# Weight sums on VectorE without GpSimd, w_in kept as float32 in DRAM and read back

## The chip, the cores and the metric

The kernel runs on one core of one Trainium2 chip. The metric is device time in microseconds (us) of one execution, the median over several. A profiled execution gives the trace. Engines are named TensorE (PE, with PEld for its weight loads), VectorE (DVE), ScalarE (ACT), GpSimd (POOL) and SyncE (SP, which issues nearly all DMAs here).

## The reference, cut to what matters

A decayed linear attention over 4 batches, 8 heads, 768 positions of 64 columns gives `x` (3072 tokens of 512 columns). Then a feed-forward block with 2048 hidden columns follows. Inputs are of float64 for the two weights, float32 else:

```
out[:, :, sl] = intra + inter                  # blocks of 64 positions, a state per head
x = attn_out.transpose(0, 2, 1, 3).reshape(B * S, H * D)
h = np.maximum(x @ w_in, 0.0)                  # 3072 x 512 @ 512 x 2048
return (h * h @ w_out).astype(np.float32)      # 3072 x 2048 @ 2048 x 512
```

## The kernel before

**Split products.** A float32 number is split in a high and a low half that TensorE takes as float32r; a product is three matmuls (high x high, high x low, low x high). So each operand is split: ScalarE copies the high half out (`gh`, `part`, `v`, ...), VectorE subtracts it for the low half (`gl` at L760, L813, L925).

**Tokens.** 24 chunks of 128 tokens. The first eight form three plain tiles of 3, 3 and 2 chunks; each goes through 16 feed-forward steps `f` (function `ffn`): a product with w_in (L742), ReLU, square, split (ScalarE L756 to L759, VectorE L760), then products with w_out for `gh` (L748, L749) and `gl` (L751). The other 16 chunks are two groups of eight, which use 7 products in place of 8 for 2 x 2 blocks of matrices (L473). Those need sums and differences of weight blocks.

**Weights.** 16 parts of w_in and 16 of w_out arrive as float64 words (`work<-w`, 512 KB each, three buffers), and `weights` converts each: ScalarE L446, VectorE L447 to L453, which leaves float32 in a buffer `m` (three of them), then the halves (ScalarE L457, VectorE L459). This takes until 128 us, beside the first two tiles.

**Differences.** `differences(i, j, key)` makes, for each pair of parts (i = 0 for w_in, 1 for w_out; j = 0 to 7), what the groups of eight need, and stores it in DRAM (`kept`, 256 KB a block). Unchanged halves are stored from where they lie (`kept<-wi`, `kept<-wo`). GpSimd adds high and low to float32 again (L800, two of 128x512) in two buffers `ob`, makes four differences (L809, 128x256), and ScalarE and VectorE split each (L812, L813) into one of four `part` buffers (`v` in the later ones). For i = 0 this may begin in the second tile, for i = 1 when the third ends. The groups' products read the blocks back by `b<-kept` (L848), six buffers ahead.

**Visits.** Attention for later chunks is done in pairs, called visits, between feed-forward steps: chunk loads (`ka<-ka`, `qv<-qv`, 512 KB), 64x64 matmuls (L473), VectorE work on the results (L522, L549 to L558, L582) and, for the groups of eight, sums of chunks (`pairs`, L834) and their halves `pa`, `pz`, `ps`, `pt` (L826, L827).

**Order.** A planner (`Plan.order`) walks through all operations with durations and keys written in the code, and of those that could start next on an engine takes the one with the smallest key. What comes out is a fixed order for each engine. At run time each engine takes its instructions in that order and waits for what each needs. A key is thus a priority, not a time: an operation whose engine is free and whose inputs are there goes at once.

The function `differences` stands for GpSimd's whole work after the tables of the first 10 us.

Of the kernel before, what the change touches and what calls it, by code (L numbers as in the profile page):

```python
# [19 lines left out]
P = 128  # L20
# [208 lines left out]
PARTED = {1: 1, 2: 1, 4: 1, 5: 1, 6: 1, 7: 1, 8: 1}  # L229
BETWEEN = {3: 3, 4: 8, 5: 12}  # L230
APART, LATER_BY = 3, 4
# [3 lines left out]
FIRST_ORDER = [1, 2, 6, 5, 7, 4, 3]  # L235
PARTS = 8
AT_ONCE = [1, 2, 4, 6, 5, 7, 3]
LAST_ORDER = [4, 1, 2, 6, 5, 7, 3]
# [44 lines left out]
def kernel(ctx: ExitStack, tc: tile.TileContext, ka, qv, lamx, w, out):  # L283
# [71 lines left out]

    kept = [tc.dram_tile([NF // 2, P, 2, 7, 2 * P], F32, name=f"kept{i}") for i in range(2)]
    make("part", REGIONS["part"][0], [2, 2 * P], F32R)
    make("b", REGIONS["b"][0], [2, 2 * P], F32R)
# [66 lines left out]
    def weights(f, i, key, load_key):  # L425
# [32 lines left out]
        oh.late = f >= F_LATE  # L458
        ol = add("DVE", tt(512), lambda: nc.vector.tensor_tensor(out=part(1), in0=at(m), in1=part(0), op=ALU.subtract), [oh], [m])  # L459
        for o in (oh, ol):  # L460
            plan.use(f"{('wi', 'wo')[i]}{f}", o)
# [13 lines left out]
    class Chunk:  # L475
# [20 lines left out]
        def load(self, key):  # L496

            def part(buf, src, ps, size):
                o = in_turn("load", plan.op("SP", LOAD, key, lambda: loaded(nc.sync.dma_start(out=at(buf)[:, ps], in_=src[self.i][:, ps]), size), [], [buf]))
                o.size, o.slack = size, SLACK * (self.i >= N_ALONE + 6)  # L500
                return o
# [277 lines left out]
    def differences(i, j, key):  # L779
# [9 lines left out]
        def store(c, n, get, deps, bufs, uses):  # L789
            stored[i, j].append(plan.op("SP", LOAD, key, lambda: nc.sync.dma_start(  # L790
                out=kept[i][j][:, :, c:c + n].rearrange("p t c k -> p t (c k)"), in_=get().bitcast(F32)), deps, bufs, lat=2.9, uses=uses))
# [4 lines left out]
        else:  # L796
            store(0, 1, lambda: flat[0][:, :, 0:2 * P], w0[:2], [], names[:1])
            store(1, 1, lambda: flat[1][:, :, 0:2 * P], w1[:2], [], names[1:])
            store(6, 1, lambda: flat[1][:, :, 2 * P:], w1[:2], [], names[1:])
        prev = [plan.op("POOL", 1.38, key, lambda r=r, a=a: nc.gpsimd.tensor_tensor(  # L800
            out=at(r), in0=a[:, 0].bitcast(F32), in1=a[:, 1].bitcast(F32), op=ALU.add), list(w[:2]), raws, gate, uses=(name,))
            for r, a, w, name in zip(raws, flat, (w0, w1), names)]

# [4 lines left out]
        for c, (out_, a, b) in zip((2, 4, 5, 3), ((0, 2, 0), (2, 3, 2), (3, 3, 0), (1, 1, 3))):  # L808
            o = plan.op("POOL", 0.84, key, lambda out_=out_, a=a, b=b: nc.gpsimd.tensor_tensor(out=side(out_), in0=side(a), in1=side(b), op=ALU.subtract), prev, raws)  # L809
            part = Buf(kind)  # L810
# [39 lines left out]
    def first_products(p, j, key):  # L850
# [20 lines left out]
        def block(k, t, f, a, deps):  # L871
            b = h[t, f]
            o = plan.op("DVE", tt(WIDE) + 0.1, key - 6, lambda: nc.vector.tensor_tensor(out=at(b), in0=at(banks[k]), in1=at(a), op=ALU.add), deps, [banks[k], b, a])  # L873
            if p == 0 and k == "z":
                made[t, f] = [plan.op("DVE", tt(WIDE) + 0.1, key, lambda: nc.vector.scalar_tensor_tensor(
                    out=at(b), in0=at(b), scalar=0.0, in1=at(b), op0=ALU.max, op1=ALU.mult), [o], [b])]
                return o
            o1 = plan.op("ACT", act(WIDE) + 0.12, key, lambda: nc.scalar.activation(at(b), at(b), AF.Relu), [o], [b])  # L878
            o1 = plan.op("ACT", act(WIDE) + 0.12, key, lambda: nc.scalar.activation(at(b), at(b), AF.Square), [o1], [b])  # L879
            made[t, f] = [o1]  # L880
            return o
# [195 lines left out]
    for i in range(2):  # L1077
        for j in range(NF // 2):
            differences(i, j, 480 + 9 * j if i == 0 else 618 + 6 * j)

# [138 lines left out]
```

## Time and profile before

| what | value |
|---|---|
| median of 3 runs | 576.63 us (575.06 to 578.34) |
| profiled execution, own time | 575.11 us |
| its span, first to last instruction | 573.3 us |
| TensorE busy | 553.9 us, 97% |
| VectorE busy | 434.5 us, 76% |
| ScalarE busy | 330.2 us, 58% |
| GpSimd busy | 103.8 us, 18% |
| mean rate of the queues | 239 GB/s |

The span is the time from the first to the last instruction; 1.8 us of the execution's own time lie around it. Busy time counts an engine's instructions without the waits before them. A matmul's recorded duration overlaps the next one's, so the busy time is that of their union. In a timeline, the idle time of the engine ahead of an instruction stands in brackets behind it, with what ended it.

### The profile page before, as it was taken

How to read it: one execution, taken by the hardware profiler on the slowest of the kernel's cores; microseconds unless marked ns; L12 is line 12 of the kernel's file. 1: busy time of each engine (PE TensorE's matmuls, PEld its weight loads, DVE VectorE, ACT ScalarE, POOL GpSimd, SP SyncE). 2: the span in 40 equal slices, each digit the busy share in tenths (PEclk: the TensorE clock that was granted, in tenths of full speed). 3: DMA queues.
4: the chain of work that ended last, by engine and by line, in shares of the span. 5: the costliest groups of instructions: out<-in, count | busy, mean ns of one | idle time of the engine just before them, and what ended most of it. 6: DMA issues, size and time to landing. Idle time of an engine off the chain costs nothing.

```text
span 573.3 us, 12872 instructions
## 1 busy us (share of the span) xinstructions
PE 553.9 (97%) x4907; PEld 468.7 (82%) x4907; DVE 434.5 (76%) x778; ACT 330.2 (58%) x676; POOL 103.8 (18%) x106
## 2 busy tenths in 40 slices
PE   8999999999989889999998999999999999999997
PEld 7898899998869778787786788888878888888885
DVE  5998999984778999867478599999822323999664
ACT  5865676763544545556565655555446767754542
POOL 3000000004574674036666000000000000000000
PEclk9999999999989999999999999999999999999999
DMA  8999799854668558589999945676776776767765
GB/s 340 348 338 288 240 285 297 288 185 157 219 232 274 158 215 300 182 274 305 361 301 344 285 137 156 196 229 193 237 243 195 191 196 191 195 191 212 215 192 183
DMA packets 104397, 137.17 MB, mean 239 GB/s; under 512 B 7056, under 2 KB 88976, under 8 KB 104336
## 3 DMA queue, kind: packets, MB, share of 16 engines
q1 hardware_dynamic: 104192, 136.34, 75.1%
q8 instruction: 39, 0.64, 0.5%
q14 instruction: 22, 0.18, 0.1%
q10 hardware_dynamic: 144, 0.01, 0.0%
HBM read 100.67 MB, written 35.65 MB: 238 GB/s over the span
## 4 chain that ended last, share of the span: by engine, by line
PE 69%; DMA 16%; DVE 9%; issue 2%; POOL 1%; ACT 1%; SPq 1%; ACTq 0%; DVEq 0%
PE bank L473 52%; PE bank L742 8%; DMA b<-kept 6%; DMA qv<-qv 4%; PE bank L751 3%; PE bank L749 3%; PE bank L748 3%; DMA ka<-ka 2%; DMA work<-w 2%; DMA work<-qv 1%; DVE part L813 1%; DVE gl L760 1%; POOL ob L800 1%; DMA out<-work 1%; DVE pa L827 1%
## 5 line engine op out<-in xcount | busy, mean ns | idle before, releaser
L473 PE MATMUL bank<-v,b 128*128 128x512 f32 x672 | 153.4, 389 | 0.0
L473 PEld LDWEIGHTS bank<-v,b 128*128 128x128 f32 x672 | 126.0, 188 | 26.3
L924 ACT CAST v<-h 128x512 fp32r<-128x512 f32 x112 | 67.4, 621 | 58.4 <-PE bank L473 36.7
L873 DVE TENSOR_TENSOR h<-bank,u 128x512 f32<-128x512 f32 x64 | 44.0, 690 | 72.1 <-ACT u L869 42.2
L925 DVE TENSOR_TENSOR v<-h,v 128x512 fp32r<-128x512 f32 x112 | 75.2, 689 | 18.9 <-ACT v L924 9.6
L473 PE MATMUL bank<-pa,b 128*128 128x512 f32 x192 | 49.4, 392 | 4.3 <-DMA b<-kept 3.4
L800 POOL TENSOR_TENSOR ob<-wi 128x512 f32<-128x512 f32 x16 | 24.3, 1534 | 152.8 <-ACT work L756 127.6
L878 ACT ACTIVATE h<-h 128x512 f32<-128x512 f32 x56 | 35.4, 632 | 28.2 <-DVE h L873 26.2
L748 PE MATMUL bank<-wo,gh 128*128 128x512 f32 x125 | 49.7, 398 | 1.6 <-ACT gh L759 1.2
L473 PE MATMUL bank<-ps,b 128*128 128x512 f32 x192 | 49.1, 391 | 0.5 <-DMA b<-kept 0.4
L749 PE MATMUL bank<-wo,gh 128*128 128x512 f32 x125 | 49.1, 393 | 0.2 <-DVE wo L459 0.2
L869 ACT COPY u<-bank 128x512 f32<-128x512 f32 x48 | 28.0, 584 | 35.4 <-PE bank L473 35.3
L473 PE MATMUL bank<-pt,b 128*128 128x512 f32 x192 | 46.7, 391 | 1.1 <-DMA b<-kept 1.1
L473 PEld LDWEIGHTS bank<-pa,b 128*128 128x128 f32 x192 | 35.6, 188 | 13.3 <-DMA b<-kept 2.6
L473 PEld LDWEIGHTS bank<-pt,b 128*128 128x128 f32 x192 | 35.8, 188 | 8.9 <-issue 1.5
L932 DVE TENSOR_TENSOR h<-h,h 128x512 f32<-128x512 f32 x64 | 42.9, 686 | 0.1
L473 PEld LDWEIGHTS bank<-ps,b 128*128 128x128 f32 x192 | 35.7, 188 | 8.8 <-ACT v L812 0.9
L742 PE MATMUL bank<-xb,wi 128*128 128x384 f32 x192 | 35.2, 336 | 0.0
L879 ACT ACTIVATE h<-h 128x512 f32<-128x512 f32 x56 | 34.4, 627 | 0.6
L742 PEld LDWEIGHTS bank<-xb,wi 128*128 128x128 f32 x192 | 33.6, 188 | 0.9
L742 PE MATMUL bank<-xa,wi 128*128 128x384 f32 x180 | 34.1, 338 | 0.0
L742 PEld LDWEIGHTS bank<-xa,wi 128*128 128x128 f32 x180 | 31.6, 188 | 1.4 <-issue 0.2
(148 smaller groups left out, 959.8 us busy)
## 6 DMA issues: line engine op xcount, KB each, us to landing
b<-kept SPq DMA_DIRECT2D x224, 256.0 KB, 3.5
work<-w SPq DMA_DIRECT2D x32, 512.0 KB, 4.8
ka<-ka SPq DMA_DIRECT2D x24, 512.0 KB, 5.3
qv<-qv SPq DMA_DIRECT2D x20, 512.0 KB, 5.9
kept<-part SPq DMA_DIRECT2D x32, 256.0 KB, 3.5
kept<-v SPq DMA_DIRECT2D x32, 256.0 KB, 5.0
kept<-wo SPq DMA_DIRECT2D x24, 256.0 KB, 3.7
kept<-wi SPq DMA_DIRECT2D x8, 512.0 KB, 4.3
```

Source lines behind the costliest of these rows:

```text
L473: nc.tensor.matmul(*args, **kw, skip_group_check=True)
L742: nc.tensor.matmul(at(h)[:, 0:n], wt[:, cc, :], xt[:, cc, :], start=k == 0, stop=k == 3 * NCC - 1)
L748: nc.tensor.matmul(at(os_[j]), at(gh)[:, sl], woh[f], start=f == 0 and ti >= SINGLE, stop=False)
L749: nc.tensor.matmul(at(os_[j]), at(gh)[:, sl], wol[f], start=False, stop=False)
L800: prev = [plan.op("POOL", 1.38, key, lambda r=r, a=a: nc.gpsimd.tensor_tensor(out=at(r), in0=a[:, 0].bitcast(F32), in1=a[:, 1].bitcast(F32 ...
L869: return plan.op("ACT", act(WIDE) + 0.09, key - 6, lambda: nc.scalar.copy(at(dst), at(banks[k])), [o], [banks[k], dst])
L873: o = plan.op("DVE", tt(WIDE) + 0.1, key - 6, lambda: nc.vector.tensor_tensor(out=at(b), in0=at(banks[k]), in1=at(a), op=ALU.add), deps, [ ...
L878: o1 = plan.op("ACT", act(WIDE) + 0.12, key, lambda: nc.scalar.activation(at(b), at(b), AF.Relu), [o], [b])
L879: o1 = plan.op("ACT", act(WIDE) + 0.12, key, lambda: nc.scalar.activation(at(b), at(b), AF.Square), [o1], [b])
L924: oh = plan.op("ACT", act(WIDE) + 0.12, key - 12, lambda: nc.scalar.copy(rounded[hi.slot], at(b)), made[t, 2 * j + e], [b, hi], after)
L925: ol = plan.op("DVE", tt(WIDE) + 0.1, key - 12, lambda: nc.vector.tensor_tensor(out=rounded[lo.slot], in0=at(b), in1=rounded[hi.slot], op= ...
L932: made[o] = [plan.op("DVE", tt(WIDE) + 0.1, when, lambda: nc.vector.tensor_tensor(out=at(h[o]), in0=at(h[a]), in1=at(h[b]), op=op), deps + ...
```

## The change

Five edits. (1) The 32 sums and 64 differences go from GpSimd to VectorE. (2) For w_in parts 4 to 15 there is no sum: the converted float32 in `m` is stored to a DRAM tensor `spare` by SP, right after conversion, and `differences` reads it back into `ob` by SP. The buffer `m` is then free only when that store has landed. (3) The stores of unchanged w_out halves get another key (520 + 12 j). (4) The last block of each run of the first group's first products (`z`) takes ReLU and square from ScalarE (two passes) in place of one VectorE pass. (5) Keys of the differences change, two visits move one feed-forward step ahead, and the planner's allowance on chunk loads holds from two chunks earlier on.

```
-BETWEEN = {3: 3, 4: 8, 5: 12}
+BETWEEN = {3: 3, 4: 7, 5: 11}
...
+D2 = 4
+SPARE_FROM, SPARE_KEY = 4, 0.0
...
+    spare, spared = tc.dram_tile([NF, P, DM], F32, name="spare"), {}
...
+        if i == 0 and f >= SPARE_FROM:
+            spared[f] = plan.op("SP", LOAD, key + SPARE_KEY, lambda: nc.sync.dma_start(out=spare[f], in_=at(m)), om, [m], lat=3.4)
...
-                o.size, o.slack = size, SLACK * (self.i >= N_ALONE + 6)
+                o.size, o.slack = size, SLACK * (self.i >= N_ALONE + 4)
...
-            stored[i, j].append(plan.op("SP", LOAD, key, lambda: nc.sync.dma_start(
+            stored[i, j].append(plan.op("SP", LOAD, 520 + 12 * j if uses and i else key, lambda: nc.sync.dma_start(
...
-        prev = [plan.op("POOL", 1.38, key, lambda r=r, a=a: nc.gpsimd.tensor_tensor(
-            out=at(r), in0=a[:, 0].bitcast(F32), in1=a[:, 1].bitcast(F32), op=ALU.add), list(w[:2]), raws, gate, uses=(name,))
-            for r, a, w, name in zip(raws, flat, (w0, w1), names)]
+        prev = []
+        for r, a, w, name, f in zip(raws, flat, (w0, w1), names, (f0, f1)):
+            if i == 0 and f in spared:
+                prev.append(plan.op("SP", LOAD, key, lambda r=r, f=f: nc.sync.dma_start(out=at(r), in_=spare[f]), [spared[f]], raws, gate, lat=3.4))
+            else:
+                prev.append(plan.op("DVE", tt(512), key, lambda r=r, a=a: nc.vector.tensor_tensor(
+                    out=at(r), in0=a[:, 0].bitcast(F32), in1=a[:, 1].bitcast(F32), op=ALU.add), list(w[:2]), raws, gate, uses=(name,)))
...
-            o = plan.op("POOL", 0.84, key, lambda out_=out_, a=a, b=b: nc.gpsimd.tensor_tensor(out=side(out_), in0=side(a), in1=side(b), op=ALU.subtract), prev, raws)
+            o = plan.op("DVE", tt(256), key, lambda out_=out_, a=a, b=b: nc.vector.tensor_tensor(out=side(out_), in0=side(a), in1=side(b), op=ALU.subtract), prev, raws)
...
-            if p == 0 and k == "z":
-                made[t, f] = [plan.op("DVE", tt(WIDE) + 0.1, key, lambda: nc.vector.scalar_tensor_tensor(
-                    out=at(b), in0=at(b), scalar=0.0, in1=at(b), op0=ALU.max, op1=ALU.mult), [o], [b])]
-                return o
...
-            differences(i, j, 480 + 9 * j if i == 0 else 618 + 6 * j)
+            differences(i, j, (470 + 30 * j if j < 4 else begin[2] + D2 * (j - 3)) if i == 0 else 614 + 8 * j)
```

Lines of the changed kernel are numbered some four or five higher: L747 for L742, L756 for L751, L765 for L760, L818 for the differences, L822 for L813, L464 for the store to `spare`, L808 for the read. Three places show how the planner's order moves.

**Conversion, SP.** SP's queue around the conversion of parts 8 and 9, before:

```order
L790 DMA kept1_160<-wo7_89 256x1x256 x2
L444 DMA work_127<-w 128x512
L790 DMA kept0_159<-wi8_74 256x1x512
L444 DMA work_127<-w 128x512
L790 DMA kept1_160<-wo8_90 256x1x256
L444 DMA work_127<-w 128x512
L790 DMA kept0_159<-wi9_75 256x1x256
```

and of the changed kernel:

```order
L795 DMA kept1_160<-wo7_89 256x1x256 x2
L447 DMA work_127<-w 128x512
L464 DMA spare_161<-work_127 128x512
L795 DMA kept0_159<-wi8_74 256x1x512
L447 DMA work_127<-w 128x512
L795 DMA kept1_160<-wo8_90 256x1x256
L464 DMA spare_161<-work_127 128x512
L447 DMA work_127<-w 128x512
L795 DMA kept0_159<-wi9_75 256x1x256
```

Twelve stores to `spare` (the buffers `m` lie in `work`) stand among the weight loads; the stores of unchanged w_out halves (`kept1<-wo`) keep their places.

**The first visit after conversion, SP and VectorE.** SP's chunk loads for it, before, and the first `part` stores behind them:

```order
L499 DMA ka_0_108<-ka 128x1024
L499 DMA qv_1_111<-qv 128x1024
L499 DMA ka_1_109<-ka 128x1024
L499 DMA work_127<-qv 128x1024
L790 DMA kept0_159<-part_0_161 256x1x256
```

and in the changed kernel:

```order
L504 DMA ka_0_108<-ka 128x1024
L504 DMA qv_1_111<-qv 128x1024
L808 DMA ob_1_107<-spare_161 128x512
L504 DMA ka_1_109<-ka 128x1024
L504 DMA work_127<-qv 128x1024
L808 DMA ob_0_106<-spare_161 128x512
L795 DMA kept0_159<-part_0_162 256x1x256
```

VectorE behind that visit's results, before:

```order
L557 TENSOR_TENSOR hold_4_122<-hold_4_122,small_132 128x256
L813 TENSOR_TENSOR part_0_161<-ob_1_107,part_0_161 128x256
L813 TENSOR_TENSOR part_1_162<-ob_0_106,part_1_162 128x256
L522 TENSOR_TENSOR qv_1_111<-qv_1_111,small_132 128x512
L813 TENSOR_TENSOR part_2_163<-ob_0_106,part_2_163 128x256
L813 TENSOR_TENSOR part_3_164<-ob_1_107,part_3_164 128x256
L760 TENSOR_TENSOR gl_1_101<-work_127,gh_1_99 128x384
```

and in the changed kernel:

```order
L562 TENSOR_TENSOR hold_4_122<-hold_4_122,small_132 128x256
L818 TENSOR_TENSOR ob_1_107<-ob_0_106,ob_1_107 128x256
L818 TENSOR_TENSOR ob_0_106<-ob_0_106 128x256
L527 TENSOR_TENSOR qv_1_111<-qv_1_111,small_132 128x512
L765 TENSOR_TENSOR gl_1_101<-work_127,gh_1_99 128x384
L818 TENSOR_TENSOR ob_0_106<-ob_0_106,ob_1_107 128x256
```

The first difference reads both `ob` buffers, so it waits for both reads of `spare`; the `gl` of a feed-forward step of the second tile stands three places behind it.

**The end of the second tile, VectorE.** The `gl` of its steps 14 and 15, before:

```order
L813 TENSOR_TENSOR part_1_162<-ob_1_107,part_1_162 128x256
L522 TENSOR_TENSOR qv_0_110<-qv_0_110,small_132 128x512
L813 TENSOR_TENSOR part_2_163<-ob_1_107,part_2_163 128x256
L813 TENSOR_TENSOR part_3_164<-ob_0_106,part_3_164 128x256
L522 TENSOR_TENSOR qv_2_112<-qv_2_112,small_132 128x512
L760 TENSOR_TENSOR gl_0_100<-work_127,gh_0_98 128x384
L760 TENSOR_TENSOR gl_1_101<-work_127,gh_1_99 128x384
```

and in the changed kernel:

```order
L822 TENSOR_TENSOR part_2_164<-ob_1_107,part_2_164 128x256
L527 TENSOR_TENSOR qv_0_110<-qv_0_110,small_132 128x512
L822 TENSOR_TENSOR part_3_165<-ob_0_106,part_3_165 128x256
L765 TENSOR_TENSOR gl_0_100<-work_127,gh_0_98 128x384
L527 TENSOR_TENSOR qv_2_112<-qv_2_112,small_132 128x512
L765 TENSOR_TENSOR gl_1_101<-work_127,gh_1_99 128x384
```

The `gl` of step 14 now stands ahead of the second chunk's `qv` product. Between the first difference of the place above and this `gl`, both counted, the changed order has 47 VectorE instructions: 11 of 512 columns, 4 of 384 and 32 of 256.

## Rows read from the trace of the kernel before

**Rows 1.** The page, busy time of the engines (us, share of span, instructions).

```profile
PE 553.9 (97%) x4907; PEld 468.7 (82%) x4907; DVE 434.5 (76%) x778; ACT 330.2 (58%) x676; POOL 103.8 (18%) x106
```

**Rows 2.** Busy time by stage, with its columns.

```profile
core 0: us, PE busy (x) PEld busy (x) DVE busy (x) ACT busy (x) POOL busy (x), PEclk, DMA share, GB/s
...
60.00:128.00 68.00, 68.00 (x346) 61.86 (x345) 65.22 (x127) 47.55 (x92) 0.00 (x0) 1.00 0.82 266
...
136.00:240.00 104.00, 96.91 (x1786) 83.97 (x1784) 90.04 (x158) 50.64 (x130) 57.38 (x54) 0.98 0.66 223
240.00:317.00 77.00, 72.20 (x769) 58.14 (x769) 54.43 (x102) 45.24 (x96) 41.09 (x42) 1.00 0.96 316
```

**Rows 3.** TensorE's waits, 136 to 245 us (total, times, longest).

```profile
PE bank L751 <- DVE gl L760: 5.8, 4, 2.5
PE bank L748 <- ACT gh L759: 1.2, 2, 0.9
PE bank L473 <- DVE pa L827: 0.9, 1, 0.9
```

**Rows 4.** TensorE's waits, 245 to 430 us.

```profile
PE bank L473 <- DMA b<-kept: 4.9, 5, 1.7
```

**Rows 5.** Timeline of TensorE: start, duration, line, tiles, idle before.

```profile
150.18 0.84 PE L751 MATMUL bank<-wo,gl 128*128 128x512 f32 x3
...
168.22 1.27 PE L751 MATMUL bank<-wo,gl 128*128 128x512 f32 x3 [2.46 <-DVE gl L760]
...
192.45 0.73 PE L751 MATMUL bank<-wo,gl 128*128 128x512 f32 x2 [1.50 <-DVE gl L760]
...
227.43 0.73 PE L751 MATMUL bank<-wo,gl 128*128 128x512 f32 x2 [0.85 <-DVE gl L760]
```

**Rows 6.** Busy time of two short stretches (columns as in rows 2).

```profile
168.70:172.00 3.30, 3.30 (x99) 2.64 (x101) 1.77 (x2) 1.92 (x7) 2.44 (x4) 0.50 0.00 0
174.80:178.40 3.60, 3.60 (x142) 3.38 (x140) 3.55 (x7) 1.79 (x4) 0.80 (x1) 1.00 1.00 354
```

**Rows 7.** VectorE by form, 136 to 240 us (busy us, mean ns, idle before).

```profile
L813 DVE TENSOR_TENSOR part<-ob,part 128x256 fp32r<-128x256 f32 x32 | 18.0, 575 | 3.9 <-ACT part L812 3.9
L760 DVE TENSOR_TENSOR gl<-work,gh 128x256 fp32r<-128x256 f32 x16 | 10.2, 634 | 1.1 <-ACT gh L759 1.1
L760 DVE TENSOR_TENSOR gl<-work,gh 128x384 fp32r<-128x384 f32 x6 | 6.3, 1045 | 4.1 <-ACT gh L759 4.1
...
L549 DVE TENSOR_TENSOR work<-bank,hold 128x256 f32<-128x256 f32 x10 | 4.1, 413 | 0.3 <-PE bank L473 0.3
```

**Rows 8.** VectorE unhindered: one form (60 to 128 us), then timeline rows.

```profile
L760 DVE TENSOR_TENSOR gl<-ob,gh 128x384 fp32r<-128x384 f32 x7 | 3.9, 552 | 0.0
...
111.60 0.69 DVE L459 TENSOR_TENSOR wi<-work,wi 128x512 fp32r<-128x512 f32 x1
112.20 0.68 DVE L451 SCALAR_TENSOR_TENSOR work<-work 128x512 uint32<-128x512 uint32 x1
...
139.90 0.41 DVE L558 TENSOR_TENSOR s<-bank,mask 128x256 f32<-128x256 f32 x1
140.23 0.41 DVE L549 TENSOR_TENSOR hold<-bank,hold 128x256 f32<-128x256 f32 x1
```

**Rows 9.** Timeline of VectorE just before two of TensorE's waits.

```profile
189.75 1.78 DVE L827 TENSOR_TENSOR pa<-xr,pa 128x512 fp32r<-128x512 f32 x1
...
226.97 0.41 DVE L760 TENSOR_TENSOR gl<-work,gh 128x256 fp32r<-128x256 f32 x1
```

**Rows 10.** DMA issues (KB each, median us to landing), 60:128 and then 136:240.

```profile
work<-w SPq DMA_DIRECT2D x18, 512.0 KB, 4.6
...
work<-qv SPq DMA_DIRECT2D x3, 512.0 KB, 6.8
```

**Rows 11.** Timeline of SP, the fourth chunk load of the visit after conversion.

```profile
141.73 0.42 SPq L499 DMA_DIRECT2D work<-qv  x1
```

**Rows 12.** Timeline of TensorE: the product with w_in part 13.

```profile
112.79 1.38 PE L742 MATMUL bank<-xa,wi 128*128 128x384 f32 x7
```

## Prediction

> **What bounds the kernel now.** I read the page's first part, then the busy time by stage, then what TensorE waited for, and last the engines it waited for. TensorE is busy for 553.9 of 573.3 us [rows 1]: no more than the 19 us between can be won, since the change adds and removes no matmul. The stages tell where these lie [rows 2]. While the weights are converted (60 to 128 us) TensorE has no gap, and VectorE is busy for 65.2 of 68 us, the queues at 0.82 share. From 136 to 240 us, the end of the second tile and the third tile, TensorE idles for 7.1 us, VectorE works for 90 of 104 us and GpSimd for 57. From 240 to 317 us TensorE idles for 4.8 us, with the queues at 0.96. After 317 us GpSimd is idle.
>
> The waits say what ended those gaps. In the third-tile stretch they are the low halves `gl` (5.8 us in four, the longest 2.5), the high halves `gh` (1.2 in two, the longest 0.9) and one `pa` (0.9), 7.9 us, all made by VectorE or behind it [rows 3]; in the next, 4.9 us are loads of `kept` [rows 4]. The 2.46 us wait costs twice: the clock granted behind it is 0.50, the lower of its two levels (1.2 of 2.4 GHz), over at least 3.3 us, in which half of the speed, 1.7 us, is lost [rows 5, 6]. The next longest, 1.50 us, can have no such stretch behind it: the one of 3.3 us by itself takes the stage's mean to the 0.98 that it has [rows 2, 5].
>
> **GpSimd's sums and differences: what they cost VectorE.** Of VectorE's instructions in that stage those with both inputs in SBUF are long: 128x256 low halves of `part` take 575 ns, 128x384 `gl` 1045. Those that read a bank stay at 413 [rows 7]. Where GpSimd is idle, a 128x384 `gl` takes 0.55 us; back to back the next instruction starts 0.60 us behind one of 512 columns and 0.33 behind one of 256 (beside 0.69 and 0.41 recorded) [rows 8], so 0.47 behind one of 384. So `part` loses 32 x (0.575 - 0.41) = 5 us, `gl` of 384 columns 6 x 0.5 = 3 us and `gl` of 256 columns 16 x 0.22 = 3.6: 12 us by these three forms. Without GpSimd they go.
>
> **What VectorE gets instead.** 20 sums (four of w_in, sixteen of w_out) x 0.60 = 12.0 us and 64 differences x 0.33 = 21.1 us, less 8 `z` passes of 512 columns (4.8) which ScalarE takes: 28 us. The third-tile stage gets only 4 sums and 32 differences, 13 us, and loses those 12 us and the stretch of the rarer forms. The stage from 240 us gets 16 sums and 32 differences, 20 us, on 54 of 77 busy [rows 2]. VectorE is not the bound on average; the question is where it comes late.
>
> **The waits, one by one.** *Those behind 185 us.* Three of `gl` (5.8 - 2.5 = 3.3 us), the longer `gh` (0.9) and the `pa` (0.9) make 5.1 us [rows 3]. Ahead of the first, of 1.50 us, VectorE spends 1.78 us on a `pa` of 512 columns that needs 0.69, and a `gl` of this kind is 0.22 long on average: 1.3 of the 1.5 us are stretch [rows 5, 7 to 9]. The next `gl` and the `gh` I read the same way, since GpSimd works through there too. The `pa` ends a visit that the change moves one step ahead, so it has a step's time more: it goes. The last `gl` wait, 0.85 us at 227, stands behind unstretched work (its `gl` took 0.41) [rows 5, 9], and the moved visit keeps that work: half of it stays. That is -4.7; as VectorE now makes differences between these `gl`, I let 0.5 come back: **-4.2**, bounds 0 and -5.1.
>
> *The 2.46 us at 168.* Here I expect no gain. In the changed order VectorE's first difference (the second order piece on VectorE) needs two reads from `spare`, the second of which SP issues behind four chunk loads. Before the change the fourth was issued at 141.73 [rows 11], and such a load lands after 6.8 us [rows 10]: 148.5. The two reads of 0.26 MB take 0.74 us each at the 354 GB/s of a full stretch [rows 6], which puts the second at 150.0. From that difference to the `gl` of step 14 the order has 47 instructions: 11 of 512 columns, 4 of 384, 32 of 256, so 11 x 0.60 + 4 x 0.47 + 32 x 0.33 = 19.0 us without a pause, until 169.0. TensorE gets to that product at 168.22 - 2.46 - 0.3 (the smaller `gh` wait, 1.2 - 0.9) = 165.5 when nothing stops it [rows 3, 5]. So it loses 3.5 us up to this point, where it lost 2.8: **+0.7**. Bounds: -2.8 if VectorE runs ahead (the reads land before TensorE's work needs them), +2 if the low halves also wait for ScalarE's copies. The loss comes in two parts, one at the first `gl` behind the reads (150.0 + 0.33 x 2 + 0.60 + 0.47 = 151.7 against TensorE at 150.2, 1.5 us) and 2 us at step 14. A part of 2 us lies between the 1.50 that kept the clock and the 2.46 that did not: I take half of the 1.7 us, **-0.8**, bounds 0 and -1.7. Later reads of `spare` stand in the order with at least a step between issue and use, and I cost them at nothing; that cover gone, each late pair costs up to 2 us.
>
> *Conversion.* Twelve stores of 256 KB go out in this stage, each from the buffer `m` of a converted w_in part, and in SP's order most stand just ahead of a load of weights (the first order piece). Each moves that load by an issue (0.4 us for such a transfer [rows 11]) and by its own transfer. 12 x 0.26 MB in 68 us are 46 GB/s on top of 266; the row's 266 GB/s at 0.82 busy share make 324 at full share [rows 2], so 312 nearly fills the queues. VectorE has 2.8 us of slack in the stage, TensorE about 1.9: the low part of w_in 13 is ready at 112.3 (111.60 + 0.69), and the product that starts at 112.79 needs it in its ninth matmul, some 1.4 us on (seven take 1.38) [rows 8, 12]. If conversion slips by VectorE's own slack, 2.8, then TensorE loses 0.9: **+0.8**, bounds 0 and, by the rival below, +11. The Trainium skill (DMA: Bandwidth & Descriptors, Specifications) puts the HBM limit of a core at about 358 GB/s. By that rule 312 leaves room and this term is 0, which would make the sum 570.8; the row, with its share of 0.82 at 266, speaks for less room, and the sum goes by the row.
>
> *The stage from 240 us.* TensorE waits for `kept` there, and the queues' work is the same but for three late stores. VectorE gets 20 us and sheds its stretch, ScalarE 16 more passes of 512 columns on 45 of 77 busy [rows 2]. I take **0**, bounds -2 (chunk loads stand ahead of `kept` loads now) and +2.
>
> *Plain output weight stores.* By the order they stand where they stood, in the conversion stage, each behind the conversion of its weight: their new place in time does not hold them back, since SP takes what is ready. That part of the change does nothing: 0.
>
> **Sum.** -4.2 + 0.7 - 0.8 + 0.8 = -3.5 from the profiled execution's 575.1 (span 573.3 and 1.8 around it): **571.6 us**. The median of the runs shown, 576.6, is 1.5 above that execution.
>
> **Rivals.** *The whole gain.* VectorE is not behind at 150 to 168 us, the clock stays up, conversion hides its stores: 575.1 - 7.9 - 1.7 = 565.5. For it: GpSimd was the reason for long `gl` in every one of the early waits. Against it: 19 us of VectorE work in a row behind a late read.
>
> *No net gain.* Late reads stop VectorE at two or three more places (2 us each), or VectorE's own sums take the place of the stretch: the 4.2 us come back, and the time is 575 to 577. For it: the in-order queue has each `gl` behind differences, and a read here takes what its neighbours of 512 KB leave. Against it: VectorE's work in the stage stays about the same (90 - 12 + 13), and none of it is stretched any more right before a `gl`. The Trainium skill (Perfetto Trace Analysis, Optimizing Scalar/DVE Operations) says the same in general, that moving work between GpSimd and VectorE might not help because they share a read port; the 575 ns of `part` agrees that they share, and only the changed run can show the rest.
>
> *Slower: the weight loads.* With three buffers, 18 loads from 60 to 128 us make six turns. If a load lands after 6.8 us, as `work<-qv` does among others, in place of 4.6 [rows 10], each turn is 2.2 us longer: 13.2 us, less the 1.9 of margin 11.3. Then 575.1 - 4.3 + 11.3 = 582. It decides from a landing of about 6.4 us. Against it: the loads are, before the change, there when VectorE comes for them, or it could not be busy for 65 of 68 us.
>
> **Chances and numbers.** The forecast (569 to 574.5) 0.41, the whole gain 0.22, no net gain 0.27, slower 0.10. About 0.5% (2.9 us, so 573.7 and 579.5) is what a measurement of this kernel can tell from no change. Faster: the gain's 0.22 and four fifths of the forecast's, 0.33: 0.55. Same: 0.08 + 0.27 = 0.35. Slower: 0.10. The range goes from 565.5 to 578.5: it leaves out the slower case and part of the whole gain, 2 in 10. The forecast's own range is 569 to 574.5.
>
> **What would show it.** Right: GpSimd idle from 10 us on; `part` at 0.41 and `gl` at 0.55 and 0.41 us throughout; `gl` waits after 185 us below 1 us in sum; a first difference on VectorE that starts near 150 us behind a read of `spare`, and a `gl` wait of about 2 us near 168. Wrong: gaps of TensorE between 60 and 136 us with weight loads above 6 us (slower); a first difference before 146 us and no wait to 170 (whole gain); idle VectorE that ends with `ob<-spare` after 180 us (no gain); more than 6 us of waits for `kept`.

## The result, and the profile after

The changed kernel takes **583.96 us** (median of 4, 582.59 to 585.33), the kernel before it 577.49 on the same chip: ratio 1.0119, 95% interval 1.0077 to 1.0161. The change makes it slower by 1.2%; predicted were 571.6 us, in a range that ends at 578.5. The profiled execution took 584.13 us, span 582.3, 9.0 us more than the one of before.

The page's busy times, then the stages (columns as in [rows 2]):

```profile
PE 556.3 (96%) x4907; PEld 471.2 (81%) x4907; DVE 432.6 (74%) x854; ACT 339.4 (58%) x692; POOL 5.3 (1%) x10
```

```profile
60.00:128.00 68.00, 66.01 (x330) 58.78 (x329) 61.88 (x123) 45.72 (x88) 0.00 (x0) 1.00 0.91 302
136.00:240.00 104.00, 91.42 (x1654) 80.02 (x1656) 70.98 (x175) 47.30 (x121) 0.00 (x0) 1.00 0.75 249
240.00:325.00 85.00, 79.02 (x912) 64.74 (x909) 70.79 (x155) 53.93 (x114) 0.00 (x0) 0.96 0.86 281
```

Against [rows 2], TensorE now idles 2.0 us in the conversion, where it had no gap, and 12.6 us from 136 to 240 us, where it idled 7.1. VectorE's busy time there fell from 90 to 71 us, and still TensorE waits more. So VectorE is not overloaded; it stands still. What TensorE waited for, in the conversion and then from 136 to 252 us:

```profile
PE bank L756 <- DVE gl L765: 0.9, 1, 0.9
PE bank L747 <- ACT wi L460: 0.6, 1, 0.6
PE bank L753 <- ACT gh L764: 0.5, 1, 0.5
```

```profile
PE bank L478 <- ACT small L693: 5.2, 2, 3.9
PE bank L756 <- DVE gl L765: 4.0, 2, 2.4
PE bank L478 <- DVE work L563: 2.2, 1, 2.2
PE bank L478 <- DVE pa L836: 1.7, 1, 1.7
```

The first output store, which follows the conversion, starts 2.4 us later than before (before, then after):

```profile
134.72 0.83 SPq L777 DMA_DIRECT2D out<-ob  x2
```

```profile
137.16 0.83 SPq L782 DMA_DIRECT2D out<-ob  x2
```

And what VectorE waited for, 140 to 260 us:

```profile
DVE ob L818 <- DMA ob<-spare: 15.0, 6, 6.8
DVE pt L836 <- ACT pt L835: 6.5, 1, 6.5
DVE gl L765 <- ACT gh L764: 5.5, 6, 2.4
```

The first line is the new one: six times, 15 us in all, the first difference of a pair (L818) stops VectorE until a read of `spare` has landed. VectorE works in order, so the `gl` and masks that TensorE wants stand behind it. Three places, on VectorE (start, duration, idle before), SP and ScalarE:

```profile
152.35 0.43 DVE L818 TENSOR_TENSOR ob<-ob,ob 128x256 f32<-128x256 f32 x1 [6.81 <-DMA ob<-spare]
```

```profile
186.33 6.70 SPq L808 DMA_DIRECT2D ob<-spare  x2
```

```profile
195.38 0.43 DVE L818 TENSOR_TENSOR ob<-ob,ob 128x256 f32<-128x256 f32 x1 [2.25 <-DMA ob<-spare]
```

```profile
238.48 0.62 ACT L835 CAST pt<-work 128x512 fp32r<-128x512 f32 x1 [6.32 <-DMA kept<-part]
```

The first pair is the one that the prediction worked out. For the third, two reads together hold SP for 6.70 us: the second waits for a buffer `ob` whose output store, issued at 185.15, lands 7.5 us later; the read goes out at 192.70 and lands at 195.29. The last row is the end of the pairs: `pt` takes the memory of `part`, and the last stores of `part`, which the order puts behind the first loads of `b`, land only then. TensorE waits 3.89 us at 235.8 for what stands behind `pt` on ScalarE, and the clock behind it and behind a later wait of 2.4 us for `kept` falls to the lower level for 3.4 us each:

```profile
239.40:242.80 3.40, 3.07 (x114) 3.07 (x118) 3.40 (x9) 1.56 (x6) 0.00 (x0) 0.50 0.04 11
283.80:287.20 3.40, 3.40 (x10) 2.64 (x8) 0.69 (x1) 1.22 (x2) 0.00 (x0) 0.50 1.07 374
```

The stretch of VectorE, on the other hand, is gone as predicted (compare [rows 7]); by form, 136 to 240 us:

```profile
L822 DVE TENSOR_TENSOR part<-ob,part 128x256 fp32r<-128x256 f32 x32 | 12.8, 416 | 0.0
...
L765 DVE TENSOR_TENSOR gl<-work,gh 128x384 fp32r<-128x384 f32 x7 | 3.9, 554 | 6.9 <-ACT gh L764 6.9
```

### The profile page after: what moved, and what is told of

It is laid out like the page before. It is cut to its first block, busy times and chain, and to the rows that moved or that the text cites. A ratio compares the mean times of both kernels' runs of the same rounds, so it can differ in the third digit from the quotient of the medians.

```text
span 582.3 us, 12909 instructions
## 1 busy us (share of the span) xinstructions
PE 556.3 (96%) x4907; PEld 471.2 (81%) x4907; DVE 432.6 (74%) x854; ACT 339.4 (58%) x692; POOL 5.3 (1%) x10
## 4 chain that ended last, share of the span: by engine, by line
PE 62%; DVE 16%; DMA 15%; issue 3%; SPq 2%; ACT 1%; DVEq 0%; ACTq 0%
PE bank L478 55%; DMA b<-kept 4%; DMA work<-w 4%; DMA ob<-spare 3%; PE bank L747 3%; DMA spare<-work 2%; DVE work L454 2%; DVE ob L818 1%; DMA out<-ob 1%; DVE work L450 1%; DVE work L456 1%; PE bank L397 1%; PE bank L756 1%; DVE part L822 1%; DMA kept<-part 1%
## 5 line engine op out<-in xcount | busy, mean ns | idle before, releaser
L883 ACT ACTIVATE h<-h 128x512 f32<-128x512 f32 x64 | 40.2, 632 | 27.1 <-DVE h L882 25.0
L884 ACT ACTIVATE h<-h 128x512 f32<-128x512 f32 x64 | 38.6, 625 | 0.4
L747 PE MATMUL bank<-xb,wi 128*128 128x384 f32 x192 | 35.2, 336 | 0.0
L747 PE MATMUL bank<-xa,wi 128*128 128x384 f32 x180 | 34.2, 339 | 0.6 <-ACT wi L460 0.6
L747 PEld LDWEIGHTS bank<-xb,wi 128*128 128x128 f32 x192 | 33.6, 188 | 0.9
L747 PEld LDWEIGHTS bank<-xa,wi 128*128 128x128 f32 x180 | 31.5, 188 | 2.4 <-ACT wi L460 1.0
L756 PE MATMUL bank<-wo,gl 128*128 128x512 f32 x80 | 24.2, 400 | 5.0 <-DVE gl L765 4.9
```

Source lines behind the costliest of these rows:

```text
L747: nc.tensor.matmul(at(h)[:, 0:n], wt[:, cc, :], xt[:, cc, :], start=k == 0, stop=k == 3 * NCC - 1)
L756: nc.tensor.matmul(at(os_[j]), at(gl)[:, sl], woh[f], start=False, stop=f == NF - 1)
```

## The experiments

Theories: **A**, reads of `spare` that land late stop VectorE (A1: because of their place on SP's queue; A2: because of the time a read takes, with two `ob` buffers for all pairs). **B**, the 12 stores delay the conversion. **C**, the order, which puts the pairs late and the last stores of `part` behind loads of `b`. **D**, VectorE is slowed by making the sums and differences at all. Ratios are to the kernel before on the same chip (its medians there 576.4, 576.9, 577.4 and 577.7 us, for e1 to e4, e5 to e8, e9 to e12, e13 to e16). A ratio is not exactly the quotient of the medians; where the two say different things, the text gives both. What is read from a trace comes from one execution; that of e10 took 588.5 us and that of e11 574.6, some 4 us above their medians.

| run | us | ratio (95%) |
|---|---|---|
| e1 no spare | 569.49 | 0.9897 (0.9849 to 0.9944) |
| e2 stores only | 575.46 | 0.9983 (0.9954 to 1.0012) |
| e3 old keys | 591.48 | 1.0265 (1.0217 to 1.0314) |
| e4 reads counted late | 586.88 | 1.0186 (1.0149 to 1.0224) |
| e5 part stores 4.4 | 568.21 | 0.9862 (0.9803 to 0.9922) |
| e6 reads on GpSimd's queue | 584.96 | 1.0127 (1.0057 to 1.0198) |
| e7 before, with stores | 578.25 | 1.0026 (0.9994 to 1.0059) |
| e8 GpSimd again, no spare | 575.02 | 0.9964 (0.9938 to 0.9990) |
| e9 reads only | 582.70 | 1.0085 (1.0050 to 1.0120) |
| e10 four reads | 584.44 | 1.0134 (1.0083 to 1.0185) |
| e11 part stores 6.0 | 570.17 | 0.9892 (0.9842 to 0.9942) |
| e12 part stores 6.5, old keys | 577.90 | 1.0005 (0.9974 to 1.0037) |
| e13 changed order, sums | 573.07 | 0.9929 (0.9891 to 0.9966) |
| e14 changed order, sums and stores | 576.60 | 0.9979 (0.9944 to 1.0014) |
| e15 order of e1, reads | 583.77 | 1.0112 (1.0060 to 1.0165) |
| e16 reads on GpSimd, 5.5 | 582.65 | 1.0086 (1.0053 to 1.0118) |

### Take `spare` away, or put GpSimd back

e1:

```diff
-SPARE_FROM, SPARE_KEY = 4, 0.0
+SPARE_FROM, SPARE_KEY = 16, 0.0
```

> No weights stored to spare and none read back: VectorE makes all 32 sums itself (12 more instructions of 512 columns, about 0.6 us each, 7.2 us), and the last stores of part stand ahead of the first loads of b. Theory A (reads of spare that arrive late stop VectorE) and theory B (the 12 stores delay the conversion): the 2.4 us of TensorE lost before 136 us, the waits of 1.6 and 2.2 us at 152 and 160 and those of 1.3 and 2.4 us at 196 and 208 go; the 3.9 us at 236 with its half clock (1.7) goes with the order: 572 to 575 us. Theory D (what costs is that VectorE makes sums and differences at all): VectorE has 7 us more to do, the low halves come later still, and the time stays at 582 to 587 us.

569.49 us, a gain of 1.0%. D falls: with 12 sums more, VectorE is as busy as before the change and TensorE idles 3.4 us in the stage. Its stage, TensorE's waits of 136 to 252 us, and two forms on VectorE:

```profile
136.00:240.00 104.00, 100.59 (x1801) 88.22 (x1800) 90.98 (x218) 52.15 (x133) 0.00 (x0) 0.97 0.71 234
```

```profile
PE bank L753 <- ACT gh L764: 2.7, 1, 2.7
PE bank L756 <- DVE gl L765: 0.7, 1, 0.7
```

```profile
L822 DVE TENSOR_TENSOR part<-ob,part 128x256 fp32r<-128x256 f32 x32 | 13.1, 419 | 2.6 <-ACT part L821 2.6
L810 DVE TENSOR_TENSOR ob<-wi 128x512 f32<-128x512 f32 x16 | 10.6, 684 | 1.0 <-DMA out<-ob 1.0
```

e8 is e1 with the sums and differences back on GpSimd:

```diff
-plan.op("DVE", tt(512), key, ... nc.vector.tensor_tensor(
+plan.op("POOL", 1.38, key, ... nc.gpsimd.tensor_tensor(
-plan.op("DVE", tt(256), key, ... nc.vector.tensor_tensor(
+plan.op("POOL", 0.84, key, ... nc.gpsimd.tensor_tensor(
```

> The kernel without spare, with sums and differences back on GpSimd: what is left of the change is the passes moved to ScalarE and the changed numbers of the planner. It tells what moving the work to VectorE is worth by itself. If the stretch of VectorE beside GpSimd is what the move removes: low halves of part are back at 0.55 us or more, gl waits of 4 to 6 us in the third tile, and 574 to 578 us, 5 to 8 us above the run without spare on VectorE. If the gain came from the planner's numbers and the passes alone: 568 to 571 us.

575.02 us. The same two kinds of low halves, where `gl` of 384 columns takes 552 ns unhindered [rows 8]:

```profile
L822 DVE TENSOR_TENSOR part<-ob,part 128x256 fp32r<-128x256 f32 x32 | 15.2, 493 | 4.5 <-ACT part L821 4.3
...
L765 DVE TENSOR_TENSOR gl<-work,gh 128x384 fp32r<-128x384 f32 x6 | 5.9, 986 | 2.4 <-ACT gh L764 2.4
```

The stretch is back (493 ns for `part` where 0.55 us or more were expected), with 6.4 us of waits for `gl` and `gh`. Moving the work to VectorE, with the order that the planner then makes, is worth 5.5 us (575.0 to 569.5; by the ratios 3.9); the planner's numbers and the passes on ScalarE are worth 0.4% beside GpSimd (0.1 to 0.6).

### The stores alone

e2 is the changed kernel with every sum on VectorE; the stores stay, nobody reads them. e7 is the kernel before with the 12 stores:

```diff
-            if i == 0 and f in spared:
+            if False and i == 0 and f in spared:
```

> The 12 stores to spare stay, nothing is read back, and VectorE makes the sums. This leaves the cost of the stores by itself, against the run without spare. Theory B: the first store of an output starts near 137.2 us as in the changed kernel, 2.4 us later than before, and the time is 2 to 3 us above the run without spare: 575 to 577 us. Rival (the stores cost nothing, the conversion slipped through something else of the change): the first output store near 134.7 us and the time as without spare. If theory D holds, 582 us or more.

```diff
+        if i == 0 and f >= 4:
+            plan.op("SP", LOAD, key, lambda: nc.sync.dma_start(out=spare[f], in_=at(m)), om, [m], lat=3.4)
```

> The kernel before, with the 12 stores to spare and nothing else of the change: theory B alone, on the other base. If the stores delay the conversion: the first store of an output starts 2 to 3 us later than the 134.7 us of before, TensorE has gaps of 1.5 to 2.5 us in sum between 60 and 136 us where it had none, and the time is 578 to 580 us. Rival: conversion has slack enough and the delay came from elsewhere: gaps below 0.5 us and 575 to 577 us.

e2 took 575.46 us: 6.0 above e1 (5.0 by the ratios). The first output store starts at 136.91 us (e1 134.58) and TensorE is busy for 66.6 of 68 us (68.0). That is 2.3 us; the rest is in its later order, a wait of 2.1 us for ScalarE's copy `u` out of a bank at 257 us and 1.7 lost at the lower clock at 275. e7 took 578.25, 1.4 above its before, its first output store 1.45 us later and two new gaps of 1.4 us in sum at 112 and 126 us; its interval includes no change. The place of the delay is that of B, its size is below what B gave.

How the stores delay the conversion shows in the changed kernel's trace. Loads of weights land after 5.4 us in place of 4.6 [rows 10], and ScalarE, which begins the conversion of a part, stands twice until a store to `spare` has landed and its buffer `m` is free (loads of 60 to 128 us, ScalarE's waits of 56 to 136 us):

```profile
work<-w SPq DMA_DIRECT2D x18, 512.0 KB, 5.4
```

```profile
ACT work L449 <- DMA spare<-work: 3.6, 2, 2.4
```

e2, e7 and e14 have the second wait too (2.9, 3.2 and 3.6 us); the kernel before and e13, without stores, have none.

### Move the reads: order, planner, queue

```diff
-... (470 + 30 * j if j < 4 else begin[2] + D2 * (j - 3)) if i == 0 else 614 + 8 * j)
+... 480 + 9 * j if i == 0 else 618 + 6 * j)
```

> The changed kernel with the keys of the differences as they were before; stores to spare and reads stay. The order puts the last stores of part ahead of the first load of b again. Theory C (the last stores of part, queued behind loads of b, hold back pt at 236 us and cost 3.9 us and the half clock behind it, 1.7): the wait on pt goes and the time falls to 577 to 579 us, while the 2.4 us of the conversion and waits behind late reads stay. Theory A alone: the reads arrive as late as they did, the wait moves to another place, and the time stays at 582 to 585 us.

591.48 us. The last stores of `part` went out ahead of the loads of `b`, `pt` came at 233.6 us in place of 238.5 and TensorE's wait behind it fell from 3.9 to 1.7 us; yet the kernel lost 7.5 us more: with the pairs earlier, waits of 3.4 us (158 us) and 4.1 (174) stand behind the reads, and 20 us in four stretches of 136 to 245 us run at the lower clock. So the place of the last stores does not carry the loss alone. The run does not clear C, though, since the old keys cost about as much without any read (e12 below); e13 decides.

```diff
-..., [spared[f]], raws, gate, lat=3.4)
+..., [spared[f]], raws, gate, lat=7.0)
```

> The changed kernel, but the planner counts 7.0 us in place of 3.4 for a read of spare to arrive, which is what the reads behind 185 us took (6.1 to 7.5). The reads move little on SP, the work behind them on VectorE moves later, and the last stores of part stand behind still more loads of b than in the changed kernel. Theory A: VectorE's idle time that ends with a read of spare (15 us) falls below 5 us, and the waits of 2.2, 1.3 and 2.4 us at 160, 196 and 208 go: 5 us less, 578 to 580 us, if the wait at 236 stays as it is. Theory C: that wait grows, to 6 us or more, and the time stays at 582 to 586 us.

586.88 us. VectorE's waits and TensorE's (136 to 260 us):

```profile
DVE ob L818 <- DMA ob<-spare: 2.3, 1, 2.3
```

```profile
PE bank L478 <- ACT pz L835: 9.5, 1, 9.5
PE bank L478 <- ACT ps L835: 2.7, 1, 2.7
```

VectorE hardly stops (2.3 us for 15.0) and the waits from 150 to 225 us are nearly gone (0.5 and 0.7 are left), as A says; but the pairs end later (the last low half of `part` at 242.7 us for 229.3), and one wait of 9.5 us takes their place, as C says. So here the reads either stop VectorE or, counted as late, make the planner end the chain of pairs later. (The 6.1 to 7.5 us of the expectation are not the range: the eight reads issued behind 185 us took 2.6 to 7.0.)

```diff
-plan.op("SP", LOAD, key, ... nc.sync.dma_start(out=at(r), in_=spare[f])
+plan.op("POOL", 1.0, key, ... nc.gpsimd.dma_start(out=at(r), in_=spare[f])
```

> The changed kernel, with the 12 reads of spare issued on GpSimd's queue in place of SP's; the stores stay on SP. SP no longer stops at a read whose buffer is in use, so chunk loads and stores of part behind it go out earlier. If SP's queue is what makes the reads late (theory A1): VectorE's idle time on reads falls from 15 us to below 6 us, and the time to 575 to 578 us. If it is the two ob buffers, which come free only when an output store or the last difference is done, and the transfer itself (theory A2): a read still takes 5 us or more from the moment its buffer is free, VectorE still idles 10 us or more, and the time stays at 580 to 586 us.

e16 does the same and counts a read at 5.5 us (`lat=5.5`, 0.55 for the issue):

> The changed kernel with the reads on GpSimd's queue and counted at 5.5 us by the planner (on that queue they took 3.0 to 8.4 us, eight of twelve between 3.3 and 5.7). If the planner's number and SP's queue together were the fault: VectorE idles less than 4 us on reads, no wait above 2 us is left in the third tile and the time is 571 to 575 us. If the chain of pairs through two ob buffers is too long with any read in it: the wait goes to pt (4 us or more) or the time stays above 579 us.

584.96 and 582.65 us. In e6 VectorE idles 7.8 us on reads, half of 15.0, in e16 3.9:

```profile
DVE gl L765 <- ACT gh L764: 9.5, 7, 2.5
DVE ob L818 <- DMA ob<-spare: 7.8, 2, 3.9
```

On a queue of their own the reads still took 3.0 to 8.4 us, two waits for `gl` of 4.4 and 4.9 us stood behind two of them in e6, and in e16 the chain ended late (`pt` at 237.6 us). A1 falls as the main cause: off SP's queue the time is that of the changed kernel (e6) or 1.3 us below it (e16). A2 stands by the time, though its 10 us of idle VectorE did not come.

### The reads alone, and fewer of them

```diff
-... nc.sync.dma_start(out=at(r), in_=spare[f]), [spared[f]], raws, gate, lat=3.4)
+... nc.sync.dma_start(out=at(r), in_=ka[f][:, 0]...), [], raws, gate, lat=3.4)
```

> The changed kernel without the 12 stores; the 12 reads stay in the order but fetch 128x512 words of the input ka, which nothing has to write first. (The sums of w_in 4 to 15 are then not sums of weights, so products made from them have other values; instructions and bytes read are those of the changed kernel.) It has the price of the reads alone. Theory A2 (a read into one of the two ob buffers takes 4 to 7 us in place of the 0.6 us that VectorE needs for a sum, and the chain of pairs ends late, at the first pt): 12 to 14 us above the kernel without spare, less what the conversion no longer loses, so 579 to 583 us, with 10 us or more of VectorE's idle time on reads or a wait of 3 us or more at pt. Rival (the reads were late only because the conversion and its stores moved everything behind by 2 us): 570 to 574 us.

The reads fetch words of the input `ka`, so only the time counts here. 582.70 us, as A2 says: the conversion is whole again (TensorE 68.0 of 68 us), VectorE idles 15.3 us on the reads and the waits of the changed kernel are there, 1.3 us below it (2.0 by the ratios).

```diff
-SPARE_FROM, SPARE_KEY = 4, 0.0
+SPARE_FROM, SPARE_KEY = 12, 0.0
```

> The changed kernel with stores and reads for w_in 12 to 15 alone: 4 in place of 12, the last two pairs. If the price goes with the number of reads: of the 14.5 us between the run without spare (569.5) and the changed kernel (584.0) a third stays, 574 to 575 us. If it is set by the end of the chain of pairs at pt, which the last two pairs make: the wait at pt stays and the time is 577 us or more. If single late reads have slack behind them: 569 to 571 us.

584.44 us, as slow as with twelve reads. The time is that of the second case, its mechanism is not: `pt` came at 220 us, in good time. Only the first of the two pairs stopped VectorE, for 5.9 us (TensorE 2.7, and 6.8 us at the lower clock); the rest is a `gh` of 5.9 us at 207, made behind stores of `part` that took up to 8.5 us, and a `gl` of 3.6 at 215, with 13.7 us at the lower clock. That is no price of four reads: order and reads had to be parted.

### One order, with and without transfers

e13 keeps the changed kernel's order; VectorE makes the sum where the read was issued, and no store goes out. e14 keeps the stores:

```diff
-... lambda r=r, f=f: nc.sync.dma_start(out=at(r), in_=spare[f]), [spared[f]], raws, gate, lat=3.4)
+... lambda r=r, a=a: nc.vector.tensor_tensor(out=at(r), in0=a[:, 0]..., in1=a[:, 1]..., op=ALU.add), [spared[f]], raws, gate, lat=3.4)
 (e13 alone)
-... lambda: nc.sync.dma_start(out=spare[f], in_=at(m)), om, [m], lat=3.4)
+... lambda: None, om, [m], lat=3.4)
```

> The changed kernel's own order on TensorE and ScalarE, with VectorE making each sum at the place where the order issues the read, and neither stores to spare nor reads. So the order written for reads is kept and their time is taken out. If the reads' and stores' time is what costs (theory A2 with B): VectorE gets 7 us more work, the waits behind late reads and at pt go, 569 to 574 us. If the order itself is what costs (theory C: pairs late in it, last part stores behind loads of b): the wait at pt and most others stay, 579 to 584 us.

> As the run before it, but the 12 stores to spare are issued (nothing reads them). The difference of these two is the price of the stores in one and the same order, and the difference to the changed kernel that of the reads. Theory B: first output store 2 us later than without the stores, 2 to 3 us more, 571 to 577 us; the reads then cost 7 to 12 us. If the order costs: 581 to 586 us, as changed.

573.07 and 576.60 us. In one and the same order the reads cost 7.4 us (584.0 - 576.6; by the ratios 8.1) and the stores 3.5 (2.9). What is left to e1, 3.6 us (1.8), is the order's, and as the intervals of e13 and e1 overlap, it is not told apart from nothing. The conversion without and with the stores, then e13's waits of TensorE, 136 to 252 us:

```profile
60.00:128.00 68.00, 68.00 (x345) 61.34 (x344) 64.49 (x126) 47.28 (x90) 0.00 (x0) 1.00 0.83 266
```

```profile
60.00:128.00 68.00, 66.07 (x330) 58.42 (x328) 62.00 (x123) 45.43 (x88) 0.00 (x0) 1.00 0.91 304
```

```profile
PE bank L478 <- DVE pa L837: 2.7, 1, 2.7
PE bank L478 <- ACT small L693: 2.5, 1, 2.5
PE bank L756 <- DVE gl L765: 0.9, 2, 0.7
PE bank L753 <- ACT gh L764: 0.3, 1, 0.3
```

The first two are behind `pt`, now at 225.8 us: these waits shrink but do not go, which is the order's part. e15 turns it round, the order of e1 with a read in place of each of 12 sums:

```diff
-... plan.op("DVE", tt(512), key, ... nc.vector.tensor_tensor(out=at(r), ...
+... plan.op("DVE", tt(512), key, ... nc.sync.dma_start(out=at(r), in_=ka[f][:, 0]...) if i == 0 and f >= 4 else nc.vector.tensor_tensor(out=at(r), ...
```

> The other way round: the order of the kernel without spare, in which 12 sums of w_in 4 to 15 are taken off VectorE and a read of 128x512 words of the input ka is issued by SP at that place (these sums are then not sums of weights). VectorE has 7 us less to do. If a read's time is what costs, whatever the order: six pairs stop VectorE for about 3 to 5 us each, 15 us or more of its idle time end with a read, and the time is 578 us or more. If VectorE's slack hides them: 568 to 572 us.

583.77 us: 14.3 more than e1 in e1's order (12.4 by the ratios). VectorE's first wait and TensorE's first, 136 to 245 and 136 to 252 us:

```profile
DVE ob L819 <- DMA ob<-ka: 20.7, 6, 7.0
```

```profile
PE bank L753 <- ACT gh L764: 9.8, 3, 6.7
```

A sum of 0.68 us became a read of 2.8 to 6.5 us, and six pairs wait 20.7 us. From the end of the first low half of `part` to that of the last the pairs take 64 us in e1 (145.4 to 209.4), 76 in e15 (145.5 to 221.9) and 74 in the changed kernel (155.0 to 229.3). In the changed order without reads they take 70 and 71 us (e13, e14), so most of the step from 64 to 74 is the order's. Against e14, `pt` comes 8.4 us later in the changed kernel (238.5 for 230.0): 4.4 us of that are there by the first low half, 3.1 come in the pairs.

### Better versions

e5 and e11 are e1 with a store of `part` counted at 4.4 and 6.0 us in place of 2.9; e12 takes 6.5 and the old keys:

```diff
-... deps, bufs, lat=2.9, uses=uses))
+... deps, bufs, lat=4.4 if bufs else 2.9, uses=uses))
```

> The kernel without spare, but the planner counts 4.4 us in place of 2.9 for a store of part to land, so that it doesn't place ScalarE's next copies into a part buffer ahead of work that TensorE waits for. In the run without spare one wait remained in the third tile, 2.7 us on gh at 199 us, with 3.4 us lost at the half clock behind it; ScalarE stood 1.7 and 1.2 us on buffers of part whose stores had not landed. If the stores' landing is its cause: both go, 6 us less, 563 to 565 us. If the wait comes from VectorE's own work: it stays or moves, 568 to 571 us.

> The kernel without spare, the planner counting 6.0 us for a store of part. Counted at 4.4 us the wait on gh at 199 us stayed (3.0 us), since the stores behind four chunk loads took 7.1 to 8.5 us. If 6.0 us moves ScalarE's copies into part behind the passes that make gh: that wait and the half clock behind it go, 564 to 567 us, and the last part stores still stand ahead of the first load of b. If the wait only moves to pt or another gl: 568 to 571 us.

> As the run before it, with 6.5 us for a store of part and the keys of the differences as they were before the change. With spare the old keys made 7.5 us more than the new ones, since the pairs stood earlier, in work that waits for them. Without spare no pair waits for a read: if that was the reason, old keys cost nothing here, and the time is 564 to 568 us; if the old keys are bad by themselves, 572 us or more.

e5: 568.21 us, the fastest median, but not told apart from e1. The wait on `gh` stayed (3.0 us at 199 us): ScalarE stands at a `part` buffer between the passes that make `gh`, since the stores issued among and behind four chunk loads take 7.3 to 8.5 us:

```profile
199.28 0.40 ACT L821 CAST part<-ob 128x256 fp32r<-128x256 f32 x1 [1.99 <-DMA kept<-part]
199.59 0.41 ACT L763 ACTIVATE work<-work 128x256 f32<-128x256 f32 x1
201.21 0.40 ACT L821 CAST part<-ob 128x256 fp32r<-128x256 f32 x1 [1.21 <-DMA kept<-part]
```

e11: 570.17. That wait went, in its profiled execution others came: 2.1 us at 223 and 3.9 for `kept` at 269, with 6.8 us at the lower clock. e12: 577.90, 7.7 above e11 (6.5 by the ratios). The old keys (and 0.5 us in a store's number) cost this without any read, so waits behind reads do not explain e3's loss by themselves: with and without reads, the change's new keys were the better ones for work on VectorE.

## Why the prediction was wrong

**The step that failed.** "Later reads of `spare` … I cost them at nothing; that cover gone, each late pair costs up to 2 us." The forecast of 0.9 us of waits behind 185 us rested on it. The cover, a step between issue and use, was not enough: from the issue of a pair's second read to VectorE's coming to its first difference lay 0.4 to 3.9 us in the five later pairs, and a read took 4.6 us in the median:

```profile
ob<-spare SPq DMA_DIRECT2D x12, 256.0 KB, 4.6
```

Of the five later pairs three stopped VectorE for over 2 us (2.25, 3.27, 2.06), and TensorE's waits of 1.34 us (196), 2.38 (208) and 3.89 (236) followed; of the last, 2.6 us are left without the reads (e14). In one order the reads, the first pair's among them, cost 7.4 us (e14). It was my rival "no net gain" in its mechanism, and its sign of idle VectorE that ends with `ob<-spare` after 180 us came true; its price was too small, since I counted single late pairs at 2 us each and not the chain of all pairs, whose end (`pt` at 238.5 us; 230.0 in e14) TensorE also needs. The changed order had no term either (3.6 us, or 1.8).

**GpSimd's work on VectorE: right.** The stretch went (416 and 554 ns), and e8 against e1 prices the move at 5.5 us (3.9) where the sum had 4.2 for the waits behind 185 us. (Its 4.7 takes the wait of 1.50 us whole, of which its own reading gives 1.3 to the stretch: 4.5.) The Trainium skill (Perfetto Trace Analysis, Optimizing Scalar/DVE Operations) warns that moving work between GpSimd and VectorE might not help because of their shared port. Here it does help: the low halves fall from 493 and 986 ns (e8) to 419 and 552 ns (e1), and the time with them.

**The 2.46 us at 168: right in place of the reads, partly in its end.** The second read landed at 152.25 us (150.0 predicted, plus the 2.4 that the conversion slipped); the first `gl` wait was 1.57 (1.5 predicted). VectorE's 47 instructions took 19.2 us (19.0). The 2 us expected at step 14 came as 2.22 us at 160, on a mask (L563), not on `gl`.

**Half clock: a hedge, and no term for later.** The sum took half of the 1.7 us back. No stretch of the third tile ran at the lower level up to 239 us, so all of it came back; then two such stretches of 3.4 us, which the sum did not have, took 3.4.

**Conversion: right in kind, too small, and one wait overlooked.** +0.8 was the term (2.8 - 1.9 is 0.9); the first output store starts 2.4 us later, and the stores cost 3.5 us by e14 against e13 (between 1.3 and 6.0 where the order differs or the base is another: e9, e7, e2). The prediction counted a store's issue and transfer ahead of a load; that the store also holds the buffer `m`, at which ScalarE stood for 3.6 us, had no term. Loads of weights land after 5.4 us in place of 4.6, below the 6.4 of the rival "slower", whose 582 us was near the result by luck. The Trainium skill's limit of about 358 GB/s (DMA: Bandwidth & Descriptors, Specifications) would have made the term 0. The stage lost 2.0 us of TensorE at a mean of 302 GB/s and a share of 0.91, so room in the mean did not hide the stores; nor was that limit a bound here, since the same kernel moved 410 GB/s from 5 to 20 us. What the bytes, the places on SP ahead of the loads and the held buffers each cost was not tried.

**From 240 us: right.** 4.2 us of waits for `kept` where there were 4.9; the lower clock behind one of them is counted above. **Plain output stores: right**, they did not move.

That two `ob` buffers are what makes a read's time count was argued from A2 and e15, not shown: a third buffer was not tried.

## What to carry to other kernels

Data that an engine can make in 0.7 us from what is on chip was not worth a DRAM round trip, whose read alone took 2.6 to 7.0 us, ahead of an in-order engine: spare engine time was there, spare latency was not. When a chain of small jobs has a late end that something else needs, count the whole chain with each transfer in it; here, hiding the transfer from one engine moved the wait to the chain's end (e4). A store costs more than its bytes: ask which buffer it holds, and who waits for that. To price a transfer, keep the order fixed and swap it for the computation, since with a planner every edit also rewrites the order.

## What the runs showed of the hardware

A read of 256 KB took from 2.6 us (issued at 192.7) to 7.0 us (issued at 186.3) in one kernel, and on GpSimd's queue 3.0 to 8.4 (e6): another queue did not shorten it. That the transfers beside it decide was not tried by itself. The length of a wait alone did not tell whether the clock falls: a wait of 2.38 us at 208 us left it at 1.00, one of 2.42 at 280 was followed by 0.50.
